# Sharing converted weight slices between two batches in an attention and two-FFN kernel

## The chip, the cores and the metric

The kernel runs on one core of a Trainium2 chip. The metric is the device time of one execution in microseconds; the time before is the median of 3 runs.

## What is computed

Causal attention with a learned decay over 4 batches of 8 heads, 576 positions and 64 columns per head; the result, as 2304 tokens of 512 columns, goes through a gated FFN (d_ff 1536), and that through a second FFN of 8 experts whose gate is balanced over tokens and experts. Shortened:

```python
scores = scale * q @ k.T + cum[:, None] - cum[None, :]   # causal; cum = cumsum(log(clip(f, 1e-4, 1)))
attn = exp(scores - max) ; x = attn / (sum(attn) + 1e-9) @ v        # 2304 x 512
x = (silu(x @ w_gate) * (x @ w_val)) @ w_out                        # first FFN, d_ff 1536
P = exp(x @ g2 - max)                                               # 2304 x 8
for _ in range(8):
    P /= P.sum(1) + 1e-9 ; P /= P.sum(0) + 1e-9 ; P *= N / E
out = sum over e of P[:, e] * (relu(x @ w1[e]) @ w2[e])             # second FFN, 8 experts, F 1024
```

All of it is float32 by the reference. The kernel splits each operand of a matmul into a high part and a rest in a reduced float32 form and sums three products (`three`, L145).

## The kernel before

Four parts run interleaved. *Attention* goes over 32 heads (`attn_unit`, L205): `load` brings q and k, casts the high parts on ScalarE and makes rests on GpSimd; `scores` multiplies, takes minima on VectorE (`mn`, L275) and exponentials on ScalarE; transposes `ps_t`, products `ps_o`; for each pair of heads, `recips` sends reciprocals through DRAM (`rd` and `rb`, L293 to L299) and `fold` (L347) scales the pair's output `bt` and splits it into `xh` and `xl`, the input of the first FFN for that batch. These lie in `xin0` for batches 0 and 2 and in `xin1` for batches 1 and 3.

*The first FFN* (`moe_unit`, L383) takes the hidden columns in 6 slices of 256. A slice has three pieces of weights (gate and value halves, and the piece for the way down), each a buffer of `wring`, which has four. For batch 0 a piece is made by `convert` (L99): it comes in as the 64-bit words of `wf`, and VectorE (L112, L115, L117, L118), ScalarE (L114, L125) and GpSimd (L123, L143) make the high part and the rest of it; the result is also stored to `wsplit` in DRAM. Batches 1 to 3 get the same pieces back by `fetch` (L136). A slice is two steps, one per half batch of 288 tokens: `up` (48 matmuls into `pm`, tanh `th` L413, two products on VectorE L414 and L415, the cast `ah` L416 and its rest `al`), and `down` of the step before (24 matmuls into `py`, added into `xa` on VectorE, L432, or copied on ScalarE for the first slice, L430). The next slice's pieces are asked for at the first half of a slice, within a batch.

`finish` (L434) ends a batch: it stores `xa` to `xd` (1152 KB, L437), and for each half makes gate logits: two casts `f` of 128x576 (L444), their rests on GpSimd, 12 matmuls `pl` (L448), a copy `ls` (L452) and a store of 9 KB to `lgd` (L453). `f` has two buffers, `ls` one of its own.

`merge` (L21) interleaves lists of steps by their costs when the program is written: batch 0's attention with the first three conversions, attention of batches 1, 2, 3 with the FFN of batches 0, 1, 2 (L476 to L479), and the last batch's FFN with `xload` of batches 0 and 1 (L520). A scheduler of the language then decides the order of instructions on each engine, from the program and its own estimate; buffers that are reused add waits.

*The second FFN* starts behind the last finish: `wload` (L531) prepares weights of a slice (`w1h`, `w1l`, `sm`, `w2h`, `w2l`), `eup` multiplies (`pa`, L579), `edown` accumulates (`py`, L631). After its first slice `gate` (L638) loads the logits from `lgd` in five pieces through one buffer `ls` (L642) and transposes them (`pz`, L646), and `balance` makes the gate weights `lg`. PSUM for the first FFN and the gate logits is a ring of three buffers (`ps_m`).

Of the kernel before, what the change touches and what calls it, by code (L numbers as in the profile page):

```python
# [33 lines left out]
def attention_two_ffns(ctx: ExitStack, tc: tile.TileContext, qkT, vt, f, wf, g2, w1, w2, out):  # L34
# [6 lines left out]
    P = 128  # L41
# [7 lines left out]
    def pool(name, bufs, **kw):  # L49
        return tc.tile_pool(name=name, bufs=bufs, **kw)  # L50
# [32 lines left out]
    xs = {}  # L83
    HB = S // 2
    NF = 7
    xd = [dram.tile([P, KD, S], F32, name=f"xd{b}") for b in range(B)]
    lgd = dram.tile([E, NT], F32, name="lgd")

# [42 lines left out]
    last_qk = [None]  # L131
    NPE = 1
    PACE = 2
    ONV = (2, 4)

    def fetch(i):  # L136
# [16 lines left out]


    at_ctx = ExitStack()
    xin0 = at_ctx.enter_context(pool("xin0", 1, side="right"))
# [34 lines left out]
    def spaces(b):  # L191
# [6 lines left out]
        if b:  # L198
            for i in range(2):
# [2 lines left out]
                nc.vector.memset(pts[1][i][:, 3, 64:128].bitcast(F32), 0.0)  # L202
                nc.vector.memset(pts[1][i][:, 4, 64:WB].bitcast(F32), 0.0)

    def attn_unit(b):  # L205
        first = b == 0
        pairs, heads = {}, {}

        def load_pair(hp):
            if hp == 0:  # L210
                xs[b] = [(xin0, xin1)[b % 2].tile([P, KD, S], F32R, tag=t, name=t) for t in ("xh", "xl")]
                if b < 2:
                    spaces(b)
            vs = vss[hp % 2]
# [132 lines left out]
        def fold(hp):  # L347
            bt = pairs[hp][1]
            rb = recips(hp)
            xh, xl = xs[b]  # L350
            nc.gpsimd.tensor_tensor(out=bt, in0=bt, in1=rb, op=ALU.mult)
            nc.scalar.copy(out=xh[:, hp], in_=bt)
            rest(xl[:, hp], bt, xh[:, hp])

# [25 lines left out]
    def group(w):  # L380
        return [w[0][:, 0], w[1][:, 0]], [w[0][:, 1], w[1][:, 1]], [w[2][:, 0], w[2][:, 1]]

    def moe_unit(b, get=fetch, ready=None):  # L383
        steps = []
        blocks = [(0, HB), (HB, HB)]
        xa = {}
        pend = []
        wts = {}

        def load(s):  # L390
            if s == 0 and ready:
                wts[s] = ready
            elif s < nsl:
                w = [get(3 * s + i) for i in range(3)]
                wts[s] = group(w)

        def up(s, bi):
            t0, n = blocks[bi]
            tk = slice(t0, t0 + n)
            xh, xl = xs[b]  # L400
            wg, wv, _ = wts[s]
            ah = actp.tile([P, 2, 288], F32R, tag="ah", name="ah")
            al = actp.tile([P, 2, 288], F32R, tag="al", name="al")
            for c in range(2):
                ps = []
                for w in (wg[c], wv[c]):
                    w4 = w.rearrange("p t (k f) -> p t k f", k=KD)
                    p1 = ps_m.tile([P, 512], F32, tag="m", name="pm")
                    three(p1[:, 0:n], [((w4[:, 0, k], w4[:, 1, k]), (xh[:, k, tk], xl[:, k, tk])) for k in range(KD)])
                    ps.append(p1[:, 0:n])  # L410
                pg, pvv = ps
                th = tmp.tile([P, 288], F32, tag="th", name="th")[:, 0:n]
                nc.scalar.activation(out=th, in_=pg, func=AF.Tanh, scale=0.5)  # L413
                nc.vector.scalar_tensor_tensor(out=th, in0=th, scalar=1.0, in1=pg, op0=ALU.add, op1=ALU.mult)  # L414
                nc.vector.tensor_tensor(out=th, in0=pvv, in1=th, op=ALU.mult)  # L415
                nc.scalar.copy(out=ah[:, c, 0:n], in_=th)  # L416
                rest(al[:, c, 0:n], th, ah[:, c, 0:n])
            pend.append((s, bi, ah, al))

        def down():  # L420
            s, bi, ah, al = pend.pop(0)
            t0, n = blocks[bi]
            _, _, wo = wts[s]
            for d in range(KD):
                ds_ = slice(d * P, (d + 1) * P)
                py = ps_m.tile([P, 512], F32, tag="m", name="py")
                three(py[:, 0:n], [((wo[c][:, 0, ds_], wo[c][:, 1, ds_]), (ah[:, c, 0:n], al[:, c, 0:n])) for c in range(2)])
                acc = xa["x"][:, d, t0:t0 + n]
                if s == 0:
                    nc.scalar.copy(out=acc, in_=py[:, 0:n])  # L430
                else:
                    nc.vector.tensor_tensor(out=acc, in0=py[:, 0:n], in1=acc, op=ALU.add)  # L432

        def finish():  # L434

            x = xa["x"]
            nc.sync.dma_start(out=xd[b], in_=x)  # L437
            for j in range(2):
                tk = slice(j * HB, (j + 1) * HB)
                pl = ps_m.tile([P, 512], F32, tag="m", name="pl")  # L440
                for i in range(2):
                    t = frm.tile([P, 2, 2, HB], F32R, tag="f", name="f")
                    src = x[:, 2 * i:2 * i + 2, tk]
                    nc.scalar.copy(out=t[:, 0], in_=src)  # L444
                    rest(t[:, 1], src, t[:, 0])
                    ops = [(ga, hl, k) for k in range(2) for ga, hl in ((gh, 0), (gh, 1), (gl, 0))]
                    for n, (ga, hl, k) in enumerate(ops):
                        nc.tensor.matmul(  # L448
                            out=pl[:, 0:HB], lhsT=ga[:, 2 * i + k], rhs=t[:, hl, k],
                            start=(i == 0 and n == 0), stop=(i == 1 and n == len(ops) - 1))  # L450
                ls = frm.tile([P, HB], F32, tag="ls", name="ls", bufs=1)
                nc.scalar.copy(out=ls[0:E], in_=pl[0:E, 0:HB])  # L452
                nc.sync.dma_start(out=lgd[:, b * S + j * HB:b * S + (j + 1) * HB], in_=ls[0:E])  # L453

        nb = len(blocks)

        def begin():
            xa["x"] = xap.tile([P, KD, S], F32, tag="xa", name="xa")
            load(0)
        steps.append((0.1, begin))  # L460
        for s in range(nsl):
            for bi in range(nb):
                def st(s=s, bi=bi):
                    if bi == 0:
                        load(s + 1)
                    up(s, bi)
                    if len(pend) > 1:
                        down()
                steps.append((blocks[bi][1] * 1.0, st))
        steps.append((10, lambda: down()))  # L470
        steps.append((20, lambda: finish()))
        return steps

    LA, LB, LC = 1.0, 1.2, 1.2
# [5 lines left out]
    at_ctx.close()  # L480

# [244 lines left out]
```

## Time and profile before

| | us |
|---|---|
| median of 3 runs | 2276.11 |
| lowest and highest | 2276.1, 2282.19 |
| the profiled execution | 2280.09 |
| its span, first to last instruction | 2278.3 |
| TensorE busy in it | 2231.7 (98%) |
| VectorE, ScalarE, GpSimd busy | 1687.7, 850.0, 883.5 |

The rows below come from that one profiled execution. Times on a row are microseconds from the start of its span; an engine counts as busy while an instruction of it runs, so that a busy TensorE may still run at less than its best rate of matmuls, and the number of matmuls in a stretch says more than the busy time. A windows row gives, behind the stretch and its length, busy time and instructions of TensorE's matmuls, of its weight loads, of VectorE, ScalarE and GpSimd, then the granted clock of TensorE as a share of its full speed, the busy share of the DMA engines and GB/s. PE is TensorE, DVE VectorE, ACT ScalarE, POOL GpSimd and SP SyncE, which issues the transfers.

### The profile page before, as it was taken

Reading aid. Unit: us, or ns where it says so; the run is one execution under the profiler, and the core shown is the slowest. Engines: PE = TensorE matmul, PEld = TensorE weight load, DVE = VectorE, ACT = ScalarE, POOL = GpSimd, SP = SyncE. Lnnn points to the kernel's source line nnn. Section 1 sums busy time; section 2 is a strip of 40 time slices with the busy share of each in tenths; the row PEclk is TensorE's granted clock in tenths of the full one; section 3 lists DMA queues with packets and bytes.
Section 4 is the critical chain, followed back from the end, with each engine's and each line's share of the span. In section 5 each row is a group of like instructions: output and inputs, shape, how many; then the busy total and the mean of one; then the engine's idle time right before and its main releaser. Section 6 shows DMA issues by size and latency. Waiting matters only on the chain.

```text
span 2278.3 us, 36224 instructions
## 1 busy us (share of the span) xinstructions
PE 2231.7 (98%) x13913; PEld 2026.4 (89%) x13913; DVE 1687.7 (74%) x3381; ACT 850.0 (37%) x1936; POOL 883.5 (39%) x668
## 2 busy tenths in 40 slices
PE   7899899999999999999999999989999999999999
PEld 5688799999999898888989989879989998898997
DVE  6778854544535798887878888886888788887876
ACT  7776754453322423322323222334222232322321
POOL 6778763342433423332323233343223232332320
PEclk9999999999999999999999999999999999999999
DMA  8766664554544211111111111121111111111101
GB/s 244 199 221 204 220 224 153 165 177 155 209 171 154 69 38 47 47 47 38 56 38 47 47 39 55 48 86 51 47 40 54 38 53 41 44 49 38 56 29 51
DMA packets 95261, 215.82 MB, mean 95 GB/s; under 512 B 9896, under 2 KB 52112, under 8 KB 83056
## 3 DMA queue, kind: packets, MB, share of 16 engines
q1 hardware_dynamic: 95088, 213.51, 29.1%
q8 instruction: 109, 1.79, 0.3%
q14 instruction: 64, 0.52, 0.1%
HBM read 184.94 MB, written 28.54 MB: 94 GB/s over the span
## 4 chain that ended last, share of the span: by engine, by line
PE 86%; DVE 6%; DMA 4%; issue 1%; ACT 1%; SPq 1%; POOL 1%; POOLq 0%; DVEq 0%; ACTq 0%
PE py L151 39%; PE pa L579 31%; PE pm L151 10%; DMA st<-wf 2%; PE ps_o L341 1%; PE ps_t L310 1%; PE ps_s L269 1%; DMA rd<-rt 1%; DVE np L275 1%; PE ps_s L273 1%; DVE al L594 1%; DVE g L115 1%; DVE xt L509 1%; PE pl L448 1%; DVE y L112 1%
## 5 line engine op out<-in xcount | busy, mean ns | idle before, releaser
L579 PE MATMUL pa<-xf,w1h 128*128 128x288 f32 x3584 | 749.7, 295 | 6.0 <-DVE c L588 6.0
L579 PEld LDWEIGHTS pa<-xf,w1h 128*128 128x128 f32 x3584 | 598.7, 188 | 44.5 <-DVE c L588 7.5
L631 DVE SCALAR_TENSOR_TENSOR acc<-py,lg,acc 128x512 f32<-128x512 f32 x531 | 395.2, 744 | 243.9 <-PE py L151 243.7
L579 PE MATMUL pa<-xf,w1l 128*128 128x288 f32 x1792 | 528.7, 295 | 0.0
L143 POOL TENSOR_TENSOR w2l<-w,w2h 128x1024 fp32r<-128x1024 f32 x64 | 155.4, 2429 | 819.7 <-ACT w2h L555 800.8
L151 PE MATMUL py<-w2h,ah 128*128 128x512 f32 x1152 | 453.8, 394 | 1.9 <-DVE acc L631 1.2
L151 PE MATMUL py<-w2l,ah 128*128 128x512 f32 x1152 | 454.3, 394 | 0.0
L151 PE MATMUL py<-w2h,al 128*128 128x512 f32 x1152 | 453.1, 393 | 0.0
L594 DVE SCALAR_TENSOR_TENSOR al<-c,ah 128x288 fp32r<-128x288 f32 x512 | 426.6, 860 | 7.6 <-ACT ah L593 6.8
L593 ACT ACTIVATE ah<-c 128x288 fp32r<-128x288 f32 x512 | 208.1, 443 | 586.0 <-PE py L151 311.4
L579 PEld LDWEIGHTS pa<-xf,w1l 128*128 128x128 f32 x1792 | 337.8, 188 | 10.7
L151 PE MATMUL pm<-xh,w 128*128 128x288 f32 x1536 | 327.5, 299 | 3.8 <-DVE th L414 2.4
L151 PEld LDWEIGHTS py<-w2h,al 128*128 128x128 f32 x1152 | 216.3, 188 | 49.9
L151 PEld LDWEIGHTS pm<-xh,w 128*128 128x128 f32 x1536 | 253.1, 189 | 6.7 <-DVE th L414 3.1
L151 PEld LDWEIGHTS py<-w2h,ah 128*128 128x128 f32 x1152 | 216.4, 188 | 30.6 <-DVE acc L631 2.7
L151 PEld LDWEIGHTS py<-w2l,ah 128*128 128x128 f32 x1152 | 216.3, 188 | 26.1
L143 POOL TENSOR_TENSOR w1l<-w,w1h 128x256 fp32r<-128x256 f32 x192 | 161.1, 865 | 186.2 <-ACT w1h L551 186.2
L151 PE MATMUL pm<-xl,w 128*128 128x288 f32 x768 | 227.2, 296 | 0.0
L599 ACT COPY m<-pa 128x288 f32<-128x288 f32 x128 | 50.3, 393 | 439.8 <-PE pa L579 437.4
L151 PE MATMUL py<-ah,w 128*128 128x288 f32 x768 | 174.2, 298 | 2.8 <-DVE xa L432 1.5
L143 POOL TENSOR_TENSOR al<-th,ah 128x288 fp32r<-128x288 f32 x96 | 84.4, 880 | 213.4 <-ACT ah L416 213.4
L143 POOL TENSOR_TENSOR w1l<-sm,w1h 128x1024 fp32r<-128x1024 f32 x64 | 155.2, 2424 | 1.4 <-ACT w1h L551 1.4
(140 smaller groups left out, 3123.3 us busy)
## 6 DMA issues: line engine op xcount, KB each, us to landing
w<-w SPq DMA_DIRECT2D x128, 512.0 KB
w<-wsplit SPq DMA_DIRECT2D x54, 1024.0 KB
qk<-qkT SPq DMA_DIRECT2D x64, 288.0 KB
st<-wf SPq DMA_DIRECT2D x18, 1024.0 KB
wsplit<-w SPq DMA_DIRECT2D x18, 1024.0 KB
cb<-cumd SPq DMA_DIRECT2D x31, 288.0 KB
xd<-xa SPq DMA_DIRECT2D x4, 1152.0 KB
xst<-xd SPq DMA_DIRECT2D x8, 576.0 KB
```

Source lines behind the costliest of these rows:

```text
L112: nc.vector.tensor_scalar(out=y, in0=top, scalar1=0x7fff, scalar2=None, op0=ALU.bitwise_and)
L115: nc.vector.scalar_tensor_tensor(out=g, in0=top, scalar=0x8000, in1=g, op0=ALU.bitwise_and, op1=ALU.bitwise_or)
L143: (eng or nc.gpsimd).tensor_tensor(out=out, in0=src, in1=hi.bitcast(F32), op=ALU.subtract)
L151: nc.tensor.matmul(out=ps, lhsT=a, rhs=b, start=(i == 0), stop=(i == n - 1))
L269: nc.tensor.matmul(out=ps[:, 0:w], lhsT=a[:, qs:qs + P], rhs=kh[:, c0:c0 + w], start=True, stop=False)
L273: nc.tensor.matmul(out=ps[:, 0:w], lhsT=a[:, qs:qs + P], rhs=kl[:, c0:c0 + w], start=False, stop=True)
L275: nc.vector.tensor_tensor_reduce(out=pt[r0:P, c0:c0 + use], in0=ps[r0:P, 0:use], in1=cb[r0:P, c0:c0 + use], scale=-SCALE, scalar=prev, op0 ...
L579: nc.tensor.matmul(out=ps, lhsT=w[:, MW[m - 1], k], rhs=x[:, m - 1, hl, k], start=(n == 0), stop=(n == len(ops) - 1))
L593: nc.scalar.activation(out=ah[:, f, tk], in_=src, func=AF.Relu)
L594: nc.vector.scalar_tensor_tensor(out=al[:, f, tk], in0=src, scalar=0.0, in1=ah[:, f, tk].bitcast(F32), op0=ALU.max, op1=ALU.subtract)
L599: nc.scalar.copy(out=m1, in_=p1)
L631: nc.vector.scalar_tensor_tensor(out=a, in0=py, scalar=lg[:, t, e:e + 1], in1=a, op0=ALU.mult, op1=ALU.add)
```

## The change

- The first FFN goes over a list of *visits*: slices 0 to 2 for batch 0 alone, slices 3 to 5 for batches 0 and 1 together (four steps each), slices 0 to 2 for batch 1, then all six for batches 2 and 3. There are still 18 conversions, in the first six visits; the fetches go from 54 to 45.
- Attention of batch 1 is merged with the first three visits, that of batch 2 with the three shared ones; one visit of batch 1 runs by itself; attention of batch 3 is merged with the rest of batch 1 and with batch 2's first slices; the last batch's FFN with `xload`, as before.
- Since batch 0's `xh` and `xl` are in use longer, batch 2's attention output is stored as it is to `x2d` in DRAM (in `fold`), and loaded, cast and split later (`recall`).
- `xa` of even batches gets a pool of its own (`xap0`).
- The pieces of the next visit are always asked for one visit ahead, over the border of a batch too (`wget`).
- `y` and `g` of a conversion have one buffer in place of two.
- `finish` makes eight casts of 128x288 per batch in place of four of 128x576, each followed by three gate matmuls; `f` still has two buffers, of half the size; `ls` takes one of the two buffers of `th`.

```diff
@@ convert
-        y = cvp.tile([P, W], U16, tag="y", name="y")
-        g = cvp.tile([P, W], U16, tag="g", name="g")
+        y = cvp.tile([P, W], U16, tag="y", name="y", bufs=1)
+        g = cvp.tile([P, W], U16, tag="g", name="g", bufs=1)
@@ attention
+    def room(b):
+        xs[b] = [(xin0, xin1)[b % 2].tile([P, KD, S], F32R, tag=t, name=t) for t in ("xh", "xl")]
+
+    def recall(b):
+        room(b)
+        xh, xl = xs[b]
+        for hp in range(KD):
+            raw_ = xl[:, hp].bitcast(F32)
+            nc.sync.dma_start(out=raw_, in_=x2d[:, hp])
+            nc.scalar.copy(out=xh[:, hp], in_=raw_)
+            rest(xl[:, hp], raw_, xh[:, hp])
...
+            if b == VIA:
+                nc.sync.dma_start(out=x2d[:, hp], in_=bt)
+                return
@@ the first FFN
+    nh = nsl // 2
+    visits = [(s, (0,) if s < nh else (0, 1)) for s in range(nsl)] + [(s, (1,)) for s in range(nh)]
+    visits += [(s, (b,)) for b in (2, 3) for s in range(nsl)]
+    orders = {b: [n for n, (_, bs) in enumerate(visits) if b in bs] for b in range(B)}
+    fresh = {(ns[0], b) for b, ns in orders.items()}
...
+    def wget(n_):
+        if n_ < len(visits):
+            get = convert if n_ < nsl else fetch
+            mw[n_] = group([get(3 * visits[n_][0] + i) for i in range(3)])
...
@@ finish
-                for i in range(2):
-                    t = frm.tile([P, 2, 2, HB], F32R, tag="f", name="f")
-                    src = x[:, 2 * i:2 * i + 2, tk]
+            for k in range(KD):
+                t = frm.tile([P, 2, HB], F32R, tag="f", name="f")
+                src = x[:, k, tk]
...
-                ls = frm.tile([P, HB], F32, tag="ls", name="ls", bufs=1)
+            ls = tmp.tile([P, HB], F32, tag="th", name="ls")
...
+    def settle(keep=0):
+        while len(pend) > keep:
+            n_, b, t0 = pend[0][:3]
+            down()
+            if n_ == orders[b][-1] and t0:
+                finish(b)
+
+    def moe_steps(lo, hi):
+        def st(n_, b, t0):
+            if t0 == 0 and b == visits[n_][1][0]:
+                wget(n_ + 1)
+            if t0 == 0 and (n_, b) in fresh:
+                xa[b] = (xap0, xap)[b % 2].tile([P, KD, S], F32, tag="xa", name="xa")
+            up(n_, b, t0)
+            settle(1)
+        return [(1.0, lambda n_=n_, b=b, t0=t0: st(n_, b, t0))
+                for n_ in range(lo, hi) for b in visits[n_][1] for t0 in (0, HB)]
@@ the merges
-    merge(attn_unit(1), moe_unit(0, convert, group(w0)), lead=LA)
-    merge(attn_unit(2), moe_unit(1), lead=LB)
-    merge(attn_unit(3), moe_unit(2), lead=LC)
+    mw[0] = group(w0)
+    merge(attn_unit(1), moe_steps(0, nh))
+    merge(attn_unit(2), moe_steps(nh, nsl), lead=1.2)
+    merge(moe_steps(nsl, nsl + 1))
+    recall(2)
+    merge(attn_unit(3), moe_steps(nsl + 1, 2 * nsl + nh), lead=1.2)
+    settle()
...
-    merge(moe_unit(3), xload(0) + xload(1))
+    merge(moe_steps(2 * nsl + nh, len(visits)), xload(0) + xload(1))
+    settle()
```

The change moves instructions on every engine. Three places follow, as the two programs have them; line numbers are those of each kernel.

ScalarE at the end of the third batch's first FFN. `f` are the casts of `finish`, `ls` the copies of its logits, `th` and `ah` belong to the last batch's steps. Before:

```order
L444 CAST f<-xa 128x576 x2
L513 CAST xf<-xst 128x2x288
L513 CAST xf<-xst 128x288
L444 CAST f<-xa 128x576
L452 COPY ls<-pl 8x288
L444 CAST f<-xa 128x576
L513 CAST xf<-xt 128x4x288
L413 ACTIVATE th<-pm 128x288
L416 CAST ah<-th 128x288
L452 COPY ls<-pl 8x288
L413 ACTIVATE th<-pm 128x288
```

and in the changed kernel:

```order
L437 CAST ah<-th 128x288
L466 CAST f<-xa 128x288 x5
L473 COPY ls<-pl 8x288
L466 CAST f<-xa 128x288 x3
L473 COPY ls<-pl 8x288
L434 ACTIVATE th<-pm 128x288
L437 CAST ah<-th 128x288
```

The casts are eight in one run in place of four among `xload`'s and a step's, and both tanh behind them use the buffers of the two `ls`.

TensorE between the last batch's gate logits (`pl`) and the second FFN (`pa`); `pz` are the transposes of `gate`. The last of `pl` in the first unbroken run, and what follows it, before:

```order
L448 MATMUL pl<-f,gl 128x288
L579 MATMUL pa<-xf,w1h 128x288 x2
L579 MATMUL pa<-xf,w1l 128x288
...
L579 MATMUL pa<-xf,w1h 128x288 x2
L579 MATMUL pa<-xf,w1l 128x288
L448 MATMUL pl<-f,gh 128x288
L579 MATMUL pa<-xf,w1h 128x288 x2
```

and in the changed kernel:

```order
L469 MATMUL pl<-f,gh 128x288 x2
L469 MATMUL pl<-f,gl 128x288
L671 MATMUL pz<-ident,ls 128x8 x8
L604 MATMUL pa<-xf,w1h 128x288 x2
L604 MATMUL pa<-xf,w1l 128x288
```

Before, 12 of the 24 `pl` stand ahead of the first `pa` and the others among them. Now all 24 stand in one run, followed by eight `pz`, and `pa` begins behind these.

SyncE at the same place. Before:

```order
L437 DMA xd_108<-xa 128x2304
L453 DMA lgd<-ls 8x288
L537 DMA w_9493<-w 128x4x256
L453 DMA lgd<-ls 8x288
L539 DMA w_9495<-w 128x2x512
L642 DMA ls<-lgd 8x512
L537 DMA w_9736<-w 128x4x256
L642 DMA ls<-lgd 8x512 x2
```

and in the changed kernel:

```order
L459 DMA xd_109<-xa 128x2304
L474 DMA lgd<-ls 8x288
L562 DMA w_9536<-w 128x4x256
L474 DMA lgd<-ls 8x288
L667 DMA ls<-lgd 8x512 x2
L564 DMA w_9538<-w 128x2x512
```

The loads of the logits for `pz` moved ahead of the second FFN's weights; they still stand behind the second store of the logits.

## Rows read from the trace of the kernel before

**Rows 1.** The page: its first line, engines, and the chain by engine.
```profile
span 2278.3 us, 36224 instructions
PE 2231.7 (98%) x13913; PEld 2026.4 (89%) x13913; DVE 1687.7 (74%) x3381; ACT 850.0 (37%) x1936; POOL 883.5 (39%) x668
...
PE 86%; DVE 6%; DMA 4%; issue 1%; ACT 1%; SPq 1%; POOL 1%; POOLq 0%; DVEq 0%; ACTq 0%
```

**Rows 2.** Windows by stage: columns as told under the table.
```profile
29.40:81.60 52.20, 43.37 (x233) 32.45 (x234) 32.06 (x97) 40.91 (x102) 40.05 (x29) 0.90 0.82 237
105.70:307.80 202.10, 188.77 (x1330) 173.00 (x1329) 163.52 (x364) 140.19 (x330) 162.82 (x129) 0.97 0.68 220
117.20:164.90 47.70, 45.02 (x333) 42.41 (x333) 33.47 (x72) 33.01 (x79) 35.04 (x30) 1.00 0.65 216
307.80:583.50 275.70, 275.70 (x2073) 266.40 (x2072) 133.57 (x364) 129.83 (x323) 97.27 (x96) 1.00 0.49 162
```

**Rows 3.** TensorE's waits in 105.7 to 307.8: us in total, times, longest.
```profile
PE ps_s L269 <- DVE mn L275: 3.0, 6, 1.2
PE pm L151 <- DVE th L414: 2.4, 3, 1.8
```

**Rows 4.** Windows: third finish, border to the second FFN, after a later idle spell.
```profile
615.00:620.00 5.00, 5.00 (x39) 5.00 (x39) 2.95 (x7) 1.79 (x3) 3.04 (x3) 1.00 0.94 351
620.00:625.00 5.00, 5.00 (x39) 4.86 (x38) 3.91 (x7) 2.95 (x6) 3.78 (x4) 1.00 0.62 217
...
760.00:765.00 5.00, 4.32 (x22) 3.38 (x21) 3.76 (x8) 3.30 (x7) 3.55 (x4) 1.00 0.50 164
...
1514.00:1518.00 4.00, 3.60 (x16) 3.60 (x16) 3.90 (x10) 1.26 (x3) 0.00 (x0) 0.57 0.17 66
```

**Rows 5.** ScalarE by line and shape, 0 to 760 us: busy, mean ns, idle before.
```profile
L416 ACT CAST ah<-th 128x288 fp32r<-128x288 f32 x96 | 41.4, 432 | 112.0 <-DVE th L415 111.9
L413 ACT ACTIVATE th<-pm 128x288 f32<-128x288 f32 x96 | 39.2, 408 | 82.4 <-PE pm L151 75.4 <-POOL al L143 6.5
...
L444 ACT CAST f<-xa 128x576 fp32r<-128x576 f32 x16 | 10.8, 674 | 6.5 <-DVE xa L432 4.5 <-issue 1.6 <-PE pl L448 0.4
...
L452 ACT COPY ls<-pl 8x288 f32<-8x288 f32 x8 | 3.1, 384 | 7.7 <-DMA lgd<-ls 7.0 <-PE pl L448 0.6
```

**Rows 6.** GpSimd by line and shape, 0 to 760 us.
```profile
L143 POOL TENSOR_TENSOR al<-th,ah 128x288 fp32r<-128x288 f32 x96 | 84.4, 880 | 213.4 <-ACT ah L416 213.4
```

**Rows 7.** Timeline of SyncE and ScalarE at the first and third finish: start, us.
```profile
315.84 0.33 SPq L437 DMA_DIRECT2D xd<-xa  x1
...
318.38 9.01 SPq L453 DMA_DIRECT2D lgd<-ls  x2
...
326.70 0.39 ACT L452 COPY ls<-pl 8x288 f32<-8x288 f32 x1 [1.43 <-DMA lgd<-ls]
...
623.16 8.87 SPq L453 DMA_DIRECT2D lgd<-ls  x2
...
631.34 0.39 ACT L452 COPY ls<-pl 8x288 f32<-8x288 f32 x1 [3.68 <-DMA lgd<-ls]
```

**Rows 8.** Timeline of ScalarE and GpSimd, first weights of the second FFN.
```profile
750.10 1.01 ACT L551 CAST w1h<-w 128x256 fp32r<-128x256 f32 x3
751.01 1.04 ACT L551 CAST w1h<-sm 128x1024 fp32r<-128x1024 f32 x1
751.96 1.04 ACT L555 CAST w2h<-w 128x1024 fp32r<-128x1024 f32 x1
...
750.56 2.25 POOL L143 TENSOR_TENSOR w1l<-w,w1h 128x256 fp32r<-128x256 f32 x3 [1.73 <-ACT w1h L551]
```

**Rows 9.** Timeline of SyncE: reciprocals written and read back.
```profile
547.06 0.29 SPq L293 DMA_DIRECT2D rd<-rt  x1
...
548.47 0.46 SPq L298 DMA_DIRECT2D rb<-rd  x1
```

More of the change, by code (lines that the diff above doesn't have):

```diff
@@ L85, in attention_two_ffns @@
     NF = 7
+    x2d = dram.tile([P, KD, S], F32, name="x2d")
     xd = [dram.tile([P, KD, S], F32, name=f"xd{b}") for b in range(B)]
@@ L133, in attention_two_ffns @@
     PACE = 2
+    VIA = 2
     ONV = (2, 4)
@@ L155, in attention_two_ffns @@
     at_ctx = ExitStack()
-    xin0 = at_ctx.enter_context(pool("xin0", 1, side="right"))
+    xa_ctx = ExitStack()
+    xin0 = xa_ctx.enter_context(pool("xin0", 1, side="right"))
+    xap0 = xa_ctx.enter_context(pool("xap0", 1, side="right"))
     cvp = at_ctx.enter_context(pool("cvp", 2, side="right"))
@@ L210, in load_pair @@
             if hp == 0:
-                xs[b] = [(xin0, xin1)[b % 2].tile([P, KD, S], F32R, tag=t, name=t) for t in ("xh", "xl")]
+                if b != VIA:
+                    room(b)
                 if b < 2:
@@ L349, in fold @@
             rb = recips(hp)
+            nc.gpsimd.tensor_tensor(out=bt, in0=bt, in1=rb, op=ALU.mult)
+            if b == VIA:
+                nc.sync.dma_start(out=x2d[:, hp], in_=bt)
+                return
             xh, xl = xs[b]
-            nc.gpsimd.tensor_tensor(out=bt, in0=bt, in1=rb, op=ALU.mult)
             nc.scalar.copy(out=xh[:, hp], in_=bt)
@@ L381, in group @@
         return [w[0][:, 0], w[1][:, 0]], [w[0][:, 1], w[1][:, 1]], [w[2][:, 0], w[2][:, 1]]
[L383 to L440, printed above, removed]
-                for i in range(2):
-                    t = frm.tile([P, 2, 2, HB], F32R, tag="f", name="f")
-                    src = x[:, 2 * i:2 * i + 2, tk]
[L444 to L450, printed above, removed]
-                ls = frm.tile([P, HB], F32, tag="ls", name="ls", bufs=1)
[L452 to L472, printed above, removed]
@@ L474, in attention_two_ffns @@
-    LA, LB, LC = 1.0, 1.2, 1.2
+    nh = nsl // 2
[3 more added lines that the diff above has]
+    fresh = {(ns[0], b) for b, ns in orders.items()}
+    pend, mw, xa = [], {}, {}
+    def wget(n_):
+        if n_ < len(visits):
+            get = convert if n_ < nsl else fetch
+            mw[n_] = group([get(3 * visits[n_][0] + i) for i in range(3)])
@@ new lines, in up @@
+    def up(n_, b, t0):
+        n = HB
+        tk = slice(t0, t0 + n)
+        xh, xl = xs[b]
+        wg, wv, _ = mw[n_]
+        ah = actp.tile([P, 2, 288], F32R, tag="ah", name="ah")
+        al = actp.tile([P, 2, 288], F32R, tag="al", name="al")
+        for c in range(2):
+            ps = []
+            for w in (wg[c], wv[c]):
+                w4 = w.rearrange("p t (k f) -> p t k f", k=KD)
+                p1 = ps_m.tile([P, 512], F32, tag="m", name="pm")
+                three(p1[:, 0:n], [((w4[:, 0, k], w4[:, 1, k]), (xh[:, k, tk], xl[:, k, tk])) for k in range(KD)])
+                ps.append(p1[:, 0:n])
+            pg, pvv = ps
+            th = tmp.tile([P, 288], F32, tag="th", name="th")[:, 0:n]
+            nc.scalar.activation(out=th, in_=pg, func=AF.Tanh, scale=0.5)
+            nc.vector.scalar_tensor_tensor(out=th, in0=th, scalar=1.0, in1=pg, op0=ALU.add, op1=ALU.mult)
+            nc.vector.tensor_tensor(out=th, in0=pvv, in1=th, op=ALU.mult)
+            nc.scalar.copy(out=ah[:, c, 0:n], in_=th)
+            rest(al[:, c, 0:n], th, ah[:, c, 0:n])
+        pend.append((n_, b, t0, ah, al))
@@ new lines, in down @@
+    def down():
+        n_, b, t0, ah, al = pend.pop(0)
+        n = HB
+        _, _, wo = mw[n_]
+        s = visits[n_][0]
+        for d in range(KD):
+            ds_ = slice(d * P, (d + 1) * P)
+            py = ps_m.tile([P, 512], F32, tag="m", name="py")
+            three(py[:, 0:n], [((wo[c][:, 0, ds_], wo[c][:, 1, ds_]), (ah[:, c, 0:n], al[:, c, 0:n])) for c in range(2)])
+            acc = xa[b][:, d, t0:t0 + n]
+            if (n_, b) in fresh:
+                nc.scalar.copy(out=acc, in_=py[:, 0:n])
+            else:
+                nc.vector.tensor_tensor(out=acc, in0=py[:, 0:n], in1=acc, op=ALU.add)
@@ new lines, in finish @@
+    def finish(b):
+        x = xa[b]
+        nc.sync.dma_start(out=xd[b], in_=x)
+        for j in range(2):
+            tk = slice(j * HB, (j + 1) * HB)
+            pl = ps_m.tile([P, 512], F32, tag="m", name="pl")
+            for k in range(KD):
+                t = frm.tile([P, 2, HB], F32R, tag="f", name="f")
+                src = x[:, k, tk]
+                nc.scalar.copy(out=t[:, 0], in_=src)
+                rest(t[:, 1], src, t[:, 0])
+                for n, (ga, hl) in enumerate(((gh, 0), (gh, 1), (gl, 0))):
+                    nc.tensor.matmul(
+                        out=pl[:, 0:HB], lhsT=ga[:, k], rhs=t[:, hl],
+                        start=(k == 0 and n == 0), stop=(k == KD - 1 and n == 2))
+            ls = tmp.tile([P, HB], F32, tag="th", name="ls")
+            nc.scalar.copy(out=ls[0:E], in_=pl[0:E, 0:HB])
+            nc.sync.dma_start(out=lgd[:, b * S + j * HB:b * S + (j + 1) * HB], in_=ls[0:E])
@@ L480, in attention_two_ffns @@
+    settle()
     at_ctx.close()
+    xa_ctx.close()
     def pool2(name, bufs, **kw):
```

## The prediction

> **What bounds the kernel now.** I read the page first: TensorE is busy 98% of the span and 86% of the chain that ended last is its own matmuls; no other engine is above 74% [rows 1]. So the sum is a sum of TensorE's idle time, and the question for every edit is where that idle time lies. The profiled execution took 2280.1 us, 1.8 of them around its span of 2278.3, and stands 4.0 us above the median of the three runs shown (2276.1); I work out a difference on it and add it to the median.
>
> Then I cut the span by stage [rows 2]. From the first batch's scores on there are two kinds of stretch. Without conversions (307.8 to 583.5 us) TensorE has no idle time at all and ends 2073 matmuls in 275.7 us, 7.52 per us; that is "full rate" below. With conversions (105.7 to 307.8 us, which is from the tenth head's scores to the 22nd's, heads counted from 0 over all batches) it ends 1330 in 202.1 us, 6.58 per us: 176.9 us of work at full rate, so 25.2 us are lost. That is the whole room of this change. The waits of that stretch [rows 3] name VectorE at scores and at the FFN's tanh products; no wait there names a DMA of weights. At the end of a batch's FFN TensorE loses nothing: at the third batch's gate logits a slice of 5 us holds 39 matmuls, full rate, and only the border to the second FFN shows 0.7 us idle [rows 4].
>
> **The change, part by part.**
>
> *Shared slices.* The diff alone suggests that the 18 conversions are drawn out. The order does not bear this out: before the 22nd head's scores stand all 18 conversions in both kernels, and 13 steps of the FFN (an up and a down of a half batch) in place of 12; with other attention work that is 129 matmuls more in the same stretch, 17.2 us at full rate, which no longer come later. What the stretch pays for them depends on its rate. At the rate of the whole stretch, 1457 matmuls take 221.4 us, 19.3 more, and the change loses 2.1 there. At the rate of its quietest piece (117.2 to 164.9 us, 333 in 47.7 us, 6.98 per us [rows 2]) they take 208.7, 6.6 more, and it gains 10.6. If the idle time swallows them whole the gain is 17.2. I take 10.6, since the quiet piece is a row with conversions and with enough steps beside them, which is what the change makes; ends −2.1 and +17.2.
>
> *The finish of the first two batches.* It moves from where FFN steps stood beside it to places with few. The 24 gate matmuls of batch 0 now stand over 2.4 heads (24.8 to 27.2) with half a step. ScalarE without the steps: its 129.8 us in the 275.7 us stretch [rows 2], less 21 steps of 1.68 (two tanh of 0.408, two casts of 0.432 [rows 5]), 16 copies into xa at the like of 0.384, and some 7 for two finishes, leave 8.1 us per head. So 2.4 heads are 19.4, eight casts at 0.43 3.4, two copies 0.8, four recalled casts at the like of 0.67 2.7: 26.3 us. TensorE's work there is about 24. If ScalarE could run without a gap, 2.3 us are lost; at the 78% that it reaches where heads run nearly alone (29.4 to 81.6 us [rows 2]) 9.6. I take **5**; below, 0, if steps beside the neighbouring heads cover it as in the 275.7 us stretch. Batch 1's stands over one head: **2** (0 to 4) in proportion.
>
> *The finish of batch 2.* Here the profile of before shows full rate [rows 4], because the four casts of 576 columns were far apart and matmuls of other kinds stood between. Now eight casts of 288 run through a ring of two buffers. A round of the ring is a cast (0.43), GpSimd's rest (like al, 0.88 [rows 6]) and three matmuls (0.40), and its rests alone are 7.0 us for eight. Between the first and the last of the 24 stand only 24 others, so TensorE has 6.4 us of work for a chain of some 9.7 (1.3 to fill, then four rounds of about 2.1): **3** lost. Then `ls` takes a `th` buffer, so the next two tanh wait until the logits have landed in DRAM. These 9 KB leave behind the 1152 KB of xd: issued at 318.4, the next user of the buffer starts at 326.7, 8.3 us; at 623.2 and 631.3, 8.2 [rows 7]. Before, only the second `ls` waited for it. The second `ls` comes some 3 us after the first, so tanh is held about 5 us; three PSUM buffers of `pm` give TensorE 4.8 us, of which part is used by then: **2**. Together **5** (3 to 7).
>
> By the Trainium skill, "DMA: Bandwidth & Descriptors", section "Anatomy of one DMA — SWDGE (gpsimd) path", a transfer costs about 2.0 us fixed and its bytes at 436 GB/s, an estimate of 2.0 us for these 9 KB; it is given for GpSimd's queue and this one is SyncE's. By it the tanh would hardly wait and the sum would be 2 us less; the trace's 8.3 us differ, and decide.
>
> *The border to the second FFN.* Before, 12 gate matmuls, 18 matmuls `pa`, and the rest spread among more `pa`; the transposes `pz` came much later. Now all 24 stand in one run, followed at once by eight `pz`. The run takes about 7.4 us of rests and hand-overs for 3.2 of work: **4** (3 to 5). The `pz` need two loads of logits through one buffer, one after the other. In SyncE's queue they stand behind the second store of logits, whose `ls` stands in ScalarE's order behind three casts of w1h, one of sm and one of w2h (1.01, 1.04, 1.04 [rows 8]), 3.1 us, of which 1.4 lie beside the last rest and matmuls. So: 1.7, the copy 0.4, two issues 0.6, two landings. A landing of a small transfer on a quiet queue is 1.4 us (rd written 547.06, read 548.47 [rows 9]): 5.5 us, of which about half a microsecond lies beside the last matmuls: **5**. At the low end, where ScalarE's casts end before the last rest and one load is early, 2; at the high end 7, with GpSimd's three rests of w1l (2.25 [rows 8]) in the queue and TensorE's clock falling after the idle spell, as in 1514 to 1518 us, where it stands at 0.57 granted (part of it at the lower of 1.2 and 2.4 GHz) and 16 matmuls take 3.6 us [rows 4]. Together **9** (5 to 12); the 0.7 us idle of before goes.
>
> *Edits at nothing.* x of batch 2 through DRAM adds 2.4 MB written and read and drops nine fetches of 1 MB; the queue does not hold TensorE in any row of the stretch [rows 3], and the four casts are counted above. Weights a slice ahead over the border of a batch: without conversions TensorE has no idle time to give back [rows 2], so nothing is gained. One buffer for y and g: VectorE does the parts of a conversion one after the other anyway; uncovered it would add one wait per conversion for GpSimd's add, in the stretch whose rate is bounded above.
>
> **Sum.** Gain 10.6 (−2.1 to 17.2); losses 5 + 2 + 5 + 9 = 21 (8 to 32); the old 0.7 back. 21 − 0.7 − 10.6 = +9.7 on 2280.1, so 2285.8 against the median 2276.1: about **2286**. Ends: 8 − 0.7 − 17.2 = −9.9, 2266; 32 − 0.7 + 2.1 = +33.4, 2310.
>
> **The rivals.**
>
> *Faster: the idle time of the conversion stretch is filled.* The extra matmuls need no VectorE result that is late, and the rate rises to 1457/202.1 = 7.21 per us; the finishes cost their low ends. Time: 2266. For it: TensorE's waits in the stretch are short ones, 3.0 us in six and 2.4 in three [rows 3], of the kind that more independent work covers. Against: even the quietest piece reaches 6.98, with VectorE at 70%. It decides from 7.1 per us upward (gain 15) with losses below 9.
>
> *No change: it does not do what it says.* The conversions stay as dense as they were; what is gained is what one step more covers, and the finishes cost about as much. Gain 10, losses 11: 2276. For it: all 18 conversions stand before the 22nd head in both orders. Against: the run of 24 gate matmuls and the eight `pz` behind it, which nothing in the order covers.
>
> *Slower still: a shared slice holds three of the four weight buffers over four steps in place of two*, so that the next slice's second and third piece are converted in a burst behind its last use, and the first step of the next slice waits for them. It decides if that burst comes with no head's work beside it; it is the −2.1 end above: with the middling losses +22, 2298. Against: heads run beside all of these steps.
>
> **How the numbers follow.** A difference of 0.3%, 6.8 us, is about what a measurement of this kernel can tell from none: below 2269.3 is faster, above 2282.9 slower. The forecast (the gain near 10.6, losses between 14 and 32: 2279 to 2297) has 0.48, of which 0.05 lies below 2282.9; the burst has 0.12; no change 0.22; faster 0.18. So slower is 0.43 + 0.12 = 0.55, within the bound 0.22 + 0.05 = 0.27, faster 0.18. The range goes from the filled stretch, 2266, to 2304, short of the top end, at which all terms would have to be at their worst at once; about 0.1 is left out on either side.
>
> **What would show it.** In the changed profile, the stretch up to the 22nd head's scores should be some 7 us longer with some 129 more matmuls (6.9 to 7.0 per us). `pl` should show idle time before it named by GpSimd's rest, for the last batch near 4 us. The first `th` after the third batch's finish should wait for the landing of lgd, and `pz` for its loads, some 5 us, perhaps with a fall of the granted clock behind it. I am wrong if that stretch runs above 7.2 per us, if TensorE's slices at the finishes stay at 39 matmuls in 5 us, or if idle time shows up at first uses of weight pieces.

## The result and the profile after

The changed kernel takes 2292.1 us (median of 6) against 2278.7 of the kernel before in the same comparison: a ratio of 1.0059, 95% interval 1.0047 to 1.0071, slower by 11 to 16 us. The forecast was 2286, its range 2266 to 2304.

The page of the changed kernel, as [rows 1]:

```profile
span 2294.5 us, 36286 instructions
PE 2233.1 (97%) x13913; PEld 2029.8 (88%) x13913; DVE 1680.3 (73%) x3381; ACT 850.8 (37%) x1952; POOL 874.7 (38%) x684
...
PE 84%; DMA 6%; DVE 4%; POOL 2%; ACT 1%; issue 1%; SPq 1%; POOLq 0%; DVEq 0%; ACTq 0%
```

The work of every engine is nearly the same, and the span is 16.2 us longer; in the chain the share of transfers went from 4 to 6%. Windows of the changed kernel: the conversion stretch, the one behind it up to 503 us, the end of attention, the third finish, the border.

```profile
104.70:316.30 211.60, 199.90 (x1451) 185.87 (x1451) 161.02 (x376) 145.58 (x350) 157.66 (x132) 0.98 0.60 191
316.30:502.80 186.50, 185.46 (x1402) 177.39 (x1400) 103.64 (x297) 106.00 (x268) 84.10 (x84) 1.00 0.49 157
515.00:545.00 30.00, 24.57 (x162) 24.00 (x161) 11.00 (x23) 9.14 (x21) 13.08 (x11) 0.89 0.54 186
620.00:640.00 20.00, 18.03 (x112) 16.39 (x112) 4.04 (x9) 5.18 (x13) 6.34 (x8) 0.91 0.37 119
750.00:770.00 20.00, 13.49 (x64) 11.05 (x63) 7.13 (x19) 7.81 (x18) 11.40 (x11) 0.66 0.31 114
```

The third finish and the border of the kernel before, to compare:

```profile
618.00:638.00 20.00, 20.00 (x152) 19.86 (x151) 7.96 (x15) 7.43 (x15) 12.88 (x10) 1.00 0.46 173
741.00:761.00 20.00, 19.62 (x140) 18.56 (x138) 17.05 (x29) 10.71 (x25) 14.46 (x12) 1.00 0.31 114
```

Against [rows 2]: 1451 matmuls in 211.6 us are 6.86 per us, where before 6.58 were. At the end of attention 162 matmuls stand where full rate gives some 225 in 30 us; the third finish and the border hold 112 and 64 where the kernel before has 152 and 140.

To compare kernels stretch by stretch I take the length of a stretch less its matmuls, each at the lower quartile of the spacing to the next matmul for its kind, over both kernels. What remains is TensorE's lost time in us, idle or at a lower clock (some even at full rate, about 0.07 per us). The border here is the 35 us from 3 us before the last batch's first `pl`.

| us lost | before | changed | forecast of the difference |
|---|---|---|---|
| start to the 10th head's scores | 55.0 | 54.5 | 0 |
| 10th to 22nd head's scores | 41.7 | 37.5 | −10.6 |
| to the third finish | 20.7 | 26.8 | +7 |
| the third finish | 0.4 | 5.6 | +5 |
| the last batch's FFN | 2.1 | 2.5 | 0 |
| the border | 2.4 | 13.3 | +8.3 |

These sum to +17.9; the rest of the second FFN gives 1.7 back, which makes the 16.2 of the spans.

TensorE's longest waits in the changed kernel that the one before does not have (us in total, times, longest):

```profile
PE ps_s L288 <- DVE pt L333: 5.1, 1, 5.1
PE pz L671 <- DMA ls<-lgd: 4.7, 1, 4.7
PE py L154 <- DVE th L436: 4.5, 2, 4.2
PE pl L469 <- POOL f L146: 3.4, 7, 1.0
```

The first belongs to the attention of batch 0, where both kernels lose 55 us in all. The second is the border's, the fourth that of the finishes, both as forecast. The third was not in the forecast. Its place, in the timeline of SyncE, VectorE and TensorE:

```profile
526.96 1.10 SPq L562 DMA_DIRECT2D w<-w  x1
...
535.00 1.45 DVE L570 TENSOR_TENSOR sm<-w 128x256 f32<-128x256 f32 x2 [2.97 <-DMA w<-w]
...
537.91 0.45 DVE L436 TENSOR_TENSOR th<-pm,th 128x288 f32<-128x288 f32 x1
...
538.41 0.61 PE L154 MATMUL py<-ah,w 128*128 128x288 f32 x1 [4.19 <-DVE th L436]
```

The sums `sm` for the second FFN's second slice stand on VectorE ahead of `th`; their weights, issued at 526.96, let them start at 535.00; the product `th` and with it `py` wait behind. Until 544 us the matmuls then run at the lower of the two clocks (0.50 granted in 538.4 to 544 us, 0.24 us apart instead of 0.13).

### The profile page after: what moved, and what is told of

Same layout as the page of the kernel before. It is cut to its first block, busy times and chain, and to the rows that moved or that the text cites. A ratio compares the mean times of both kernels' runs of the same rounds, so it can differ in the third digit from the quotient of the medians.

```text
span 2294.5 us, 36286 instructions
## 1 busy us (share of the span) xinstructions
PE 2233.1 (97%) x13913; PEld 2029.8 (88%) x13913; DVE 1680.3 (73%) x3381; ACT 850.8 (37%) x1952; POOL 874.7 (38%) x684
## 4 chain that ended last, share of the span: by engine, by line
PE 84%; DMA 6%; DVE 4%; POOL 2%; ACT 1%; issue 1%; SPq 1%; POOLq 0%; DVEq 0%; ACTq 0%
PE py L154 39%; PE pa L604 31%; PE pm L154 10%; DMA st<-wf 2%; PE ps_o L360 1%; PE ps_t L329 1%; DMA rd<-rt 1%; DMA xst<-xd 1%; DVE xt L533 1%; DMA cb<-cumd 1%; PE ps_s L292 1%; PE ps_s L288 1%; DVE al L619 1%; DVE np L294 0%; DMA qk<-qkT 0%
## 5 line engine op out<-in xcount | busy, mean ns | idle before, releaser
L619 DVE SCALAR_TENSOR_TENSOR al<-c,ah 128x288 fp32r<-128x288 f32 x512 | 419.1, 845 | 14.4 <-ACT ah L618 13.2
```

The source lines that it names most:

```text
L619: nc.vector.scalar_tensor_tensor(out=al[:, f, tk], in0=src, scalar=0.0, in1=ah[:, f, tk].bitcast(F32), op0=ALU.max, op1=ALU.subtract)
```

## The experiments

All are compared with the kernel before; the changed kernel stands at 1.0059. "Sharing" is the change's two-batch slices.

**1. The finish alone, in the kernel before.** The edit is the diff's part on `finish`: eight casts, and `ls` from `th`.

> The kernel before, with the change's finish alone (eight casts of 128x288, ls in a buffer of th). Theory: the finish makes the two largest losses of the change, so this kernel shows the run of 24 pl followed by pz at the border (some 11 us lost between the last py of the first FFN and steady pa, before 2.9) and some 5 us at the third batch's finish, and nothing of the sharing: slower than before by 12 to 17 us, near 2293. Rival (the sharing is what costs, through the longer tail of FFN steps without attention): within 4 us of before, near 2280.

2302.2 us, ratio 1.0108 (1.0088 to 1.0128): slower by some 24 us, even above what was expected; its profiled execution, the fastest of its runs, shows 13.1 us lost at the border and 7.8 at the third finish. The rival falls: the finish alone costs more than the whole change does. Its two halves are taken apart in experiments 5 and 6.

**2. The change without sharing.**

```diff
-    visits = [(s, (0,) if s < nh else (0, 1)) for s in range(nsl)] + [(s, (1,)) for s in range(nh)]
+    visits = [(s, (b,)) for b in (0, 1) for s in range(nsl)]
...
-    merge(attn_unit(1), moe_steps(0, nh))
-    merge(attn_unit(2), moe_steps(nh, nsl), lead=1.2)
-    merge(moe_steps(nsl, nsl + 1))
+    merge(attn_unit(1), moe_steps(0, nsl))
+    merge(attn_unit(2), moe_steps(nsl, 2 * nsl), lead=1.2)
     recall(2)
-    merge(attn_unit(3), moe_steps(nsl + 1, 2 * nsl + nh), lead=1.2)
+    merge(attn_unit(3), moe_steps(2 * nsl, 3 * nsl), lead=1.2)
...
-    merge(moe_steps(2 * nsl + nh, len(visits)), xload(0) + xload(1))
+    merge(moe_steps(3 * nsl, len(visits)), xload(0) + xload(1))
```

> The changed kernel with every slice converted for batch 0 alone and batch 1 served afterwards; finish, x2d, recall and the lead over batch borders stay. Theory: border and finishes still cost 11 and 5 to 8 us, the gain of about 4 us in the conversion stretch goes, and so does the 8 us stall of TensorE behind VectorE near the end of attention, if that stall comes from where attention ends: 2286 to 2298. Rival (sharing is what costs): back at the kernel before, 2276 to 2282.

1.0067 (1.0051 to 1.0083): as the changed kernel. Sharing is not what costs; 13.6 us are still lost at the border and 4.2 at the third finish. The stall at 515 to 545 us is gone (1.6 lost there), but 6.7 us are lost at 310 to 330, for a reason that experiment 10 shows; that the two kernels stand level is in part a coincidence of these two.

**3. `pz` held back.** `gate` and `balance` one slice later, with

```diff
+            with tc.issue_after(last_w[0].ins):
                 nc.sync.dma_start(out=ls[:, 0:n], in_=lgd[:, t0:t0 + n])
...
+                with tc.issue_after(last_pa[0].ins):
                     nc.tensor.transpose(pz[:, t * E:(t + 1) * E], ls[:, t * P:(t + 1) * P], ident[0:E, 0:E])
```

where `issue_after` lets an instruction or transfer go only behind the one named, `last_w` is the last load of w2 and `last_pa` the last `pa` so far.

> The changed kernel with the transposes pz and their loads of logits held back on their engines until the second slice of the second FFN. Theory: the 4.7 us wait of pz for ls<-lgd goes, and with it most of the spell at a granted clock of 0.52; the hand-overs of the 24 pl stay (some 3 us). Faster than the changed kernel by 5 to 8 us: 2284 to 2287. Rival (the wait only stands in for the second store of the logits or for the weights of the second FFN, which pa needs anyway): pa waits in its place, within 2 us of 2292.

1.0107 (1.009 to 1.0125), 10 us slower still than the changed kernel: a miss, and the most useful run. The border lost about as much as in the changed kernel (some 13 us by the table's measure), with other names (waits of TensorE, then VectorE's timeline):

```profile
PE pa L606 <- DVE u L615: 3.3, 1, 3.3
PE pa L606 <- ACT m L626: 1.7, 1, 1.7
...
758.27 1.67 DVE L572 TENSOR_TENSOR sm<-w 128x256 f32<-128x256 f32 x2 [12.17 <-DMA w<-w]
759.87 0.44 DVE L615 TENSOR_TENSOR u<-pa,m 128x288 f32<-128x288 f32 x1
```

With `pz` gone, `pa` waits for `u`, which stands on VectorE behind sums `sm`; their weights are issued at 754.74 us, right behind GpSimd's three rests `w1l` (752.61 to 754.71). The rival's wait came, then, and its time did not: two waits end at the border almost together, and neither alone is the price. The other 11 us were lost at 880 to 910 us, where the balancing now comes a slice later and `py` and `pa` wait for VectorE (2.6 and 2.2 us).

**4. The first two w1 loads held back.**

```diff
+        with tc.issue_after(last_dma[0].ins) if i < 2 else ExitStack():
             nc.sync.dma_start(out=st, in_=w1[e][:, c0:c0 + FS].rearrange("(k p) f -> p k f", p=P))
```

> The changed kernel with the first two w1 loads of the second FFN held behind the last load of xst. Theory: in the changed kernel the sums sm of the second slice's w1 stand on VectorE ahead of th and wait for their load, so that TensorE loses 4.2 us at py and runs at a clock of 0.78 after it; held back, that place (515 to 550 us) loses 2 to 3 us instead of 9: faster by 5 to 8 us, 2284 to 2287, if nothing is given back at the border. Rival (py waits there for its own th in any case, since attention's last reciprocals hold GpSimd and ScalarE): within 2 us of 2292.

1.0044 (1.0029 to 1.0059), about 3 us better than the changed kernel, less than the 5 to 8 expected. At the place of the stall nothing is left, and a part comes back later, where the same sums now stand among `xload`'s on VectorE:

```profile
515.00:545.00 30.00, 30.00 (x228) 29.95 (x227) 9.92 (x22) 8.42 (x19) 9.87 (x10) 1.00 0.48 171
720.00:730.00 10.00, 7.45 (x45) 7.21 (x44) 7.35 (x14) 2.53 (x3) 9.48 (x7) 0.83 0.37 111
```

The stall at 515 to 545 is shown to be the loads' place; its rival falls.

**5 to 9. One line.** Experiment 3 raised the question why no `pa` stands among the `pl` to cover these waits. The order in which the first `u` and `c` of the second FFN stand on VectorE in the two programs, with the semaphores that they wait for (Activation is ScalarE's, DVE VectorE's own, DMAHW a transfer's), gave an answer to test. Changed kernel:

```
1004 L613 TENSOR_TENSOR u_9213<-pa,m_9204 128x288 [waits Activation_49]
1005 L613 TENSOR_TENSOR c<-pa,m_9204 128x288 [waits DMAHW2_49,DVE_49]
```

and before:

```
1006 L588 TENSOR_TENSOR u_9170<-pa,m_9161 128x288 [waits Activation_49]
1007 L588 TENSOR_TENSOR c<-pa,m_9161 128x288 [waits DVE_49]
```

The first `c` now waits for a transfer. In the built programs the two buffers of `th` lie at bytes 64800 to 67104 of a partition, and the second FFN's `u3` and `c` at 64288 to 66592 and 66592 to 68896. With `ls` as the last thing in `th`, the store of the logits must have read it before `u3` or `c` is written there. Before, `ls` lay under `acc`, which is written later.

In the trace no engine is seen to wait for that store itself. What differs is the order: in the changed kernel `u` and `c` stand behind two sums `sm` that wait for weights, and run at 765.38 and 765.75 (their rows are under "Why the prediction was right"). Before, they stand right behind the last `xa`, 20 us earlier:

```profile
744.68 0.46 DVE L588 TENSOR_TENSOR u<-pa,m 128x288 f32<-128x288 f32 x1
745.05 0.45 DVE L588 TENSOR_TENSOR c<-pa,m 128x288 f32<-128x288 f32 x1
```

That the scheduler puts them later because of the added wait is inferred; that the place of `ls` makes the difference is what these kernels test.

```diff
-                ls = frm.tile([P, HB], F32, tag="ls", name="ls", bufs=1)
+                ls = tmp.tile([P, HB], F32, tag="th", name="ls")
```

in the kernel before, all else as it was:

> The kernel before with one line of the change: ls takes one of the two buffers of th; the casts stay four of 128x576. Theory: the border's loss comes from this line, since th's two buffers lie at addresses 64800 to 67104 of a partition, where the second FFN keeps u3 (64288 to 66592) and c (66592 to 68896); with ls there last, the first u3 and c, and so the first slice's pa, wait for the stores of the logits. So 24 pl in one run, about 10 us lost more at the border, little elsewhere: 2286 to 2291. Rival (the eight casts of 128x288 make the run): no more than 3 us over before.

1.005 (1.0037 to 1.0062), +11.7 us from one line; 11.1 us lost at the border. The other half, eight casts with `ls` as before:

> The kernel before with the other half of the new finish: eight casts of 128x288, ls in its own buffer. Theory: the border keeps pa between the pl and loses no more than before; the third batch's finish loses 3 to 7 us through the ring of two: 2281 to 2286. Rival (the casts make the border's run): 2288 or more.

1.0032 (1.002 to 1.0045), +7.8: 5.7 lost at the third finish, 3.0 at the border. The longest wait at this third finish is one of `pa` for a cast of `xload` (1.9 us), which stands among the casts `f` here. The line reversed, in the changed kernel (`ls` back in `frm`):

> The changed kernel with ls in a buffer of its own again, all else unchanged. Theory: pl and pa interleave again at the border, the wait of pz (4.7 us), the spell at a clock of 0.52 and some of the hand-overs go: 9 to 11 us faster than the changed kernel, 2281 to 2284, still a little slower than before through the stall near the end of attention and the third finish. Rival (the border waits for w1l and the load of the third w1 in any case): no more than 3 us faster.

1.0000 (0.9989 to 1.0011), 2276.7 us: better than expected, all of the loss is gone. The third finish and the border, to set beside 112 and 64 matmuls:

```profile
612.00:632.00 20.00, 19.24 (x140) 18.52 (x140) 5.36 (x12) 5.99 (x15) 7.37 (x10) 1.00 0.47 148
...
738.00:758.00 20.00, 19.40 (x131) 17.68 (x130) 13.42 (x28) 11.65 (x29) 12.27 (x12) 1.00 0.23 87
```

The stall at the end of attention went too, though nothing in this edit names it: the first w1 is issued at 530 us instead of 515 in this program's order. Both together:

> The changed kernel with ls in its own buffer and the first two w1 loads held behind the last load of xst. Theory: the gains of both add, 9 to 11 and some 4 (holding the loads back alone gained 4): 2277 to 2280, level with before, what is left being the third finish (5) against the conversion stretch (4). Rival (with pa free to start, late w1 loads stall the border instead): 2283 or more.

1.0013 (1.0003 to 1.0022), 2280.3 us: worse than `ls` alone. The gains do not add, because the stall that the second edit removes was no longer there, and its cost among `xload`'s sums was (3.2 us lost at 720 to 740).

To separate the ring of `th` from the place in memory, `ls` got a third buffer behind the two of `th`, `tmp.tile([P, HB], F32, tag="ls", name="ls", bufs=1)`:

> The changed kernel with ls in a buffer of its own that lies at 67104 to 68256, behind the two of th, where the second FFN's c will be (66592 to 68896). Theory (the border waits because of what lies over ls later, not because of the ring of th): 24 pl in one run and pz behind, the border loses 10 to 13 us as in the changed kernel, and the third finish, where th no longer waits for ls, loses 1 to 3: 2284 to 2290. Rival (the ring of th is the cause, as the prediction had it): as with ls in its own pool, 2275 to 2279.

1.0026 (1.0017 to 1.0035). The border loses 13.3 us, exactly as in the changed kernel, while the third finish loses 1.9 as with `ls` in `frm`. TensorE's waits at the border of this kernel, as in the changed one:

```profile
PE pz L671 <- DMA ls<-lgd: 4.9, 1, 4.9
PE pl L469 <- POOL f L146: 1.5, 4, 0.5
```

So the place in memory makes the border's loss, and in the changed kernel the ring of `th` most of the third finish's: with `ls` in it no tanh stands between the casts of `finish`; with `ls` elsewhere one does (620.16 us in experiment 7), and a second stands ahead of the last `ls`. The ring is not a price by itself. In the kernel before, with its four casts, it costs little there (1.4 lost in experiment 5), and eight casts without it lose as much as the changed kernel (5.7 in experiment 6), among casts of `xload`.

| us lost | 10th to 22nd head | to third finish | third finish | border |
|---|---|---|---|---|
| before | 41.7 | 20.7 | 0.4 | 2.4 |
| changed | 37.5 | 26.8 | 5.6 | 13.3 |
| before, `ls` in `th` | 40.9 | 23.8 | 1.4 | 11.1 |
| before, eight casts | 42.5 | 20.3 | 5.7 | 3.0 |
| changed, `ls` in `frm` | 37.5 | 19.4 | 1.9 | 3.0 |
| changed, `ls` behind `th` | 37.8 | 18.9 | 1.9 | 13.3 |
| no sharing, `ls` in `frm` | 34.7 | 30.4 | 1.9 | 3.0 |
| four slices alone | 34.1 | 19.8 | 1.9 | 2.9 |

**10 to 12. What the sharing is worth, and a faster version.** Experiment 2 with `ls` in `frm`:

> Without sharing, and with ls in its own buffer: the new finish's casts, x2d, recall and the lead over borders remain. Theory: the sharing is worth about the 4 us that the conversion stretch gained in the changed kernel, against some 2 lost at the first two finishes, so this kernel is 0 to 6 us slower than the shared one with ls in its own buffer (2276.7): 2277 to 2283. Rival (the sharing is worth the 10.6 that the prediction gave it): 2287 or more.

1.0023 (1.0011 to 1.0035), some 5 us above experiment 7, as expected. But that is not the worth of sharing. This kernel keeps `recall`, which nothing but sharing needs, and here its loads stand at the first finish: ScalarE waits for one ahead of the casts `f`, and TensorE's `pl` for these.

```profile
317.27 0.67 ACT L220 CAST xh<-xl 128x576 fp32r<-128x576 f32 x1 [5.80 <-DMA xl<-x2d]
317.84 0.76 ACT L466 CAST f<-xa 128x288 fp32r<-128x288 f32 x2
...
318.32 0.61 PE L469 MATMUL pl<-f,gh 128*128 128x288 f32 x1 [3.87 <-ACT f L466]
```

At 310 to 330 us it loses 8.3 us, experiment 7 loses 1.4: 6.9 of the 7.9 us between the two profiled spans. The same wait (4.9 us) stands in experiment 2. In the conversion stretch the kernel without sharing does no worse than the shared one, by the rate (6.90 per us) or by the table (34.7 us lost against 37.5), and it has as many steps there (26 tanh in both, 24 before):

```profile
101.40:308.00 206.60, 197.06 (x1425) 182.54 (x1423) 162.25 (x378) 145.86 (x344) 169.32 (x138) 0.98 0.67 219
```

So what the change gains in that stretch comes from a part that both kernels have, and which one no run shows; that sharing is worth anything is not shown.

Rests of `finish` on VectorE (`rest(t[:, 1], src, t[:, 0], nc.vector)`), with sharing and `ls` in `frm`:

> The changed kernel with ls in its own buffer and the rests of finish on VectorE, about half as long as on GpSimd. Theory: with the ring no longer a wall (third finish 0.2 to 2 us lost) little is left to gain, 0 to 3 us, from the border's last hand-overs and GpSimd's w1l: 2273 to 2277. Rival (VectorE at the border is late with the sums and c already): 2278 or more.

0.999 (0.998 to 0.9999): some 2 us below the kernel before, hardly clear of experiment 7. And four slices alone, two shared:

```diff
-    nh = nsl // 2
+    nh = 4
```

> The changed kernel with ls in its own buffer, and four slices converted for batch 0 alone, two shared. Theory: sharing fewer slices leaves conversions denser in the second batch's attention, and the value of the sharing is small anyway: between the shared kernel with ls own (2276.7) and the one without sharing, within 4 us of 2278. Rival (three is a sharp optimum because attention of the third batch then has its conversions): 2284 or more.

0.9982 (0.9971 to 0.9993), 2273.5 us: 4 us faster than before and the largest gain, though 0.2% is less than the 0.3% that the prediction took as the least to be told from none. Its conversion stretch has 1498 matmuls in 214.3 us, 6.99 per us:

```profile
100.60:314.90 214.30, 205.61 (x1498) 191.70 (x1497) 166.08 (x382) 151.32 (x357) 167.06 (x136) 0.98 0.63 204
```

Why four is better than three is not settled; the profile shows only that more steps stand beside the same 18 conversions (28 tanh in place of 26), and that less sharing costs nothing.

## Why the prediction was right

The direction held, and the border and the third finish cost about what was forecast. The gain in the conversion stretch was less than half and has another cause, and one stall was not foreseen. The sum was closer than its parts, and that was luck: the missing gain (6.4 us) and the stall (7) alone make 13 us, and smaller losses in other places took most of it back, so that the forecast of +9.7 is 3.6 short of the +13.3 of the medians.

- *Conversion stretch*, −10.6 forecast. The extra matmuls came (1451 for 1457), at 6.86 per us, between the two rates weighed; the stretch took 9.5 us more rather than 6.6, and lost 4.2 us less than before (6.6 by the forecast's own count at 7.52 per us). The mis-sized step is the choice of the quietest piece's rate. The step before it, that the shared slices bring the matmuls into this stretch, failed: without sharing the stretch holds 1425 at 6.90 per us (experiment 10). The forecast's 1330 and 129 make 1459, not 1457; nothing hangs on it.
- *The first two finishes*, +7. Their stretches (360 to 400 and 495 to 515 us) lost 8.6 us where some 4.4 are usual at full rate: about 4. Of `recall` the forecast counted the casts but not the wait for the loads, for which ScalarE stands 1.8 us here and 5.8 in experiment 10.
- *The third finish*, +5: measured 5.2. Its parts were not as told, so the size is luck. The chain of casts was to cost 3 and leaves 1.9 with `ls` elsewhere. No tanh waited for a landing: the first starts 0.3 us after the second `ls`, at 632.35, and the second, in that `ls`'s buffer, starts at 635.37 and waits for TensorE. So the store issued at 632.47 held its buffer for 2.9 us at most, where the forecast took 8.3. The ring of `th` costs through the order, which experiment 9 puts at 3.7 of the 5.6 lost.
- *The border*, +8.3: measured 10.9. The run of 24 `pl` takes 7.9 us (forecast 7.4), though its waits for GpSimd's rests are 1.5 and not near 4; from 756 us on it runs at the lower clock. The matmuls behind the wait for `ls` run at the lower clock until 770 us, which costs some 2 us (an estimate: 20 of them, 0.24 us apart in place of 0.13); the forecast had that at its high end alone. The chain came as written: in the timeline, engine by engine, `w1h` at 757.22, the second `ls` at 760.03, its store and the loads behind it, `pz` at last.

```profile
757.22 1.01 ACT L576 CAST w1h<-w 128x256 fp32r<-128x256 f32 x3
...
760.03 0.38 ACT L473 COPY ls<-pl 8x288 f32<-8x288 f32 x1
...
760.77 0.35 SPq L474 DMA_DIRECT2D lgd<-ls  x1
761.21 4.00 SPq L667 DMA_DIRECT2D ls<-lgd  x2
...
764.36 0.56 PE L671 MATMUL pz<-ident,ls 8*128 8x8 f32 x4 [4.74 <-DMA ls<-lgd]
...
763.91 1.55 DVE L570 TENSOR_TENSOR sm<-w 128x256 f32<-128x256 f32 x2 [4.06 <-DMA w<-w]
765.38 0.45 DVE L613 TENSOR_TENSOR u<-pa,m 128x288 f32<-128x288 f32 x1
765.75 0.44 DVE L613 TENSOR_TENSOR c<-pa,m 128x288 f32<-128x288 f32 x1
```

  But the step that gave the price to `pz` and its loads was wrong as a cause: experiment 3 took them away and `pa` waited as long (3.3 and 1.7 us against 4.7) for VectorE and ScalarE. The cause is under both, the place of `ls` in memory (experiments 5, 7 and 9), and the prediction had taken the line on `ls` for a matter of the tanh's buffers alone.
- *Missing*: about 7 us at 515 to 545 us, VectorE's sums for the second FFN ahead of `th`. The forecast listed nothing for weights of the second FFN that come earlier relative to the first; it was in the order (the second `sm` waits for a transfer, and `th` is behind it).
- *The other rivals.* The filled stretch did not come: it needed 7.1 per us. "No change" fell with the measured time. A burst at a slice's first use does not show among the waits.

A change with `ls` left in its place would have been no slower than before (experiment 7); that is the rival "no change", with another reason than the one given.

## What to carry to other kernels

When a tile moves to another pool, ask what a later stage keeps at its address: the last user of a buffer at a stage's end decides when the next stage may write there, and here one line that put a small store last there cost 11.7 us. Where two waits end together, removing the one that the profile names only shows the other; test the common cause. When an experiment takes a part of a change away, look whether what is left of it still makes sense: a helper that served only the part removed can cost more than the part gave. And price a step from the order on each engine around it, also for work of a later stage that the scheduler has pulled ahead of it.

## What the hardware showed beyond the expected

- Two sums of 128x256 on VectorE take 0.76 us together at 518.76 us, where GpSimd is idle, and 1.45 at 535.00 and 1.55 at 763.91, where GpSimd's multiplication or rests run beside them; at 535.00 that added to the wait on the way to `th`. No run separates GpSimd from the transfers beside them.
- Behind the two long waits TensorE ran at a lower granted clock: 0.89 mean in 515 to 545 us (0.50 in 538.4 to 544) and 0.66 in 750 to 770 (0.55 in 764.3 to 770.2). Some 2 us of each stall were paid after the wait had ended. At the border the clock had fallen already among the `pl` (0.78 in 752 to 759 us), whose single waits are at most 0.5 us.
